# First two feed-forward blocks of chunk 0 filled by quarters of 128 tokens

## The chip, the cores and the metric

The kernel runs on one core of a Trainium2 chip. The metric is device time in microseconds (us), from the start of the program to its end; a time "of the kernel" is the median of several executions. TensorE (PE) does the matmuls, VectorE (DVE) and ScalarE (ACT) read its results out of PSUM, GpSimd (POOL) works in SBUF only, SyncE (SP) issues transfers. Transfers are issued by SP, ACT and POOL; those of POOL can change the type on the way (float32 in memory to bf16 in SBUF), those of SP and ACT do not.

## The reference

Attention with a decay and a causal mask over 8 batches, 8 heads, 576 positions, 64 per head; its output is the input of a gated feed-forward network over all 4608 tokens.

```python
# attention, q k v: (8, 8, 576, 64), s: (8, 8, 576), all float32
scores = q @ k.T / sqrt(64)
cum = cumsum(max(s, 0), axis=-1)
scores = where(causal, -1e9, scores + min(-(cum_q - cum_k), 0))
attn = softmax(scores)                       # with + 1e-9 in the denominator
x = (attn @ v) as (4608, 512)                # heads side by side
# feed-forward: w_gate, w_val (512, 1536), w_out (1536, 512), rms_g (512)
xn = x / sqrt(mean(x * x) + 1e-6) * rms_g
out = (silu(xn @ w_gate) * (xn @ w_val)) @ w_out
```

## The kernel before

**Two pipelines laid into each other.** The feed-forward runs over 9 chunks of 512 tokens (function `ffn(c)`). Within a chunk it goes over 12 blocks (fb) of 128 of the 1536 inner features. For a block, four matmuls make the gate bank Gp (L946) and four the val bank Vp (L955), each 128 x 512 in PSUM and summed over the 512 inputs. ScalarE computes Tanh of the gate (tile T, L949); VectorE makes U = (T + 1) * Gp (L958) and Ht = U * Vp (L951). Then four row tiles of output are made from the 12 blocks (L972), copied out by ScalarE and stored. Gate, val and output banks, and some others, come from one ring of four PSUM banks (`psF`); a bank is free again when U (gate) or Ht (val) has read it. Further banks: `psS` (two), `psAV` and `psT`, one each.

Between the groups of matmuls `ffn` calls `step()`, which advances a counter, the **slot** (36 per chunk, two per block and three per row tile of output). In each slot a planner in the code (not on the chip) places a piece of attention for the tokens that come next: S (scores of 128 keys by 256 queries, then Exp on ScalarE and a mask on POOL), AV (attention times v, followed on VectorE by the division into x_sb), T (transposes of q and k by TensorE, four 128x128 matmuls and a copy) and XT (the transposes of scaled x into xnT). The functions `can_s`, `can_av`, `can_t` say from which slot on a piece may be placed. Transfers, casts and checks stand in queues (`v_side`, `pool_side`, `act_side`, `dve_side`); `put(queue, n, ...)` lets an entry run from slot n on. All of it becomes one fixed order of instructions per engine, and each engine works through its own strictly in order.

**The beginning.** Batch 0 is done ahead of chunk 0 in an order written out by hand: loads, casts to bf16, transposes, scores, AV for quarters 0 to 3 of 128 tokens, each followed by the sum of squares (`norms`, ScalarE) and `alpha` (POOL: the factor 1/rms). Then, with TensorE kept busy by filler matmuls whose results nobody reads (`warm`, L849): for each quarter qb, `x_scale` (VectorE, L484) writes xs_sb, `do_xt` transposes it on TensorE into a psF16 bank (L504) and ScalarE copies it into xnT (L511), followed by two filler matmuls. Then come g_row (a copy by ScalarE), `check_mag` and two `check_max` of q of batch 0 on VectorE (L516, L522, a running maximum for a check of the value range), a one-element memset into wg_sb on VectorE (L1206), and chunk 0. Gate matmuls of chunk 0 read all four quarters of xnT.

**Loads around it.** v of batch 0 comes in five pieces; `fold_v` multiplies each with its decay factor (POOL, L417). Weights come by `load_w(src, dst, f0, f1)` from POOL, blocks f0 to f1: gate 0 to 4 and val 0 to 6 ahead of the first x, gate 4 to 6 behind the last `alpha`, gate 6 to 12 at slot 1 (behind the memset L1206, which writes into its place), val 6 to 9 and 9 to 12 at slot 3, w_out at slot 11. q and k of batch 1 come as float32 into kq32 through SP (L137) in four transfers of 512 KB: k and q of heads 0 to 3, then k and q of heads 4 to 7, behind four one-element memsets on VectorE (L1183). They are cast to bf16 (kqn) from slot 2 on: k of heads 0 to 3 on ScalarE (slot 2, L151), q of heads 0 to 3 on POOL (slot 4, L153), then heads 4 to 7 on both (slots 6 and 9). The transposes T of batch 1 (L203) follow two slots behind the cast that they need.

The three lines that tie an entry to a slot:

```python
def put(queue, n, *fns):
    queue.extend((lambda: slot[0] >= n, f) for f in fns)
put(act_side, 2, lambda: (piece1(ACT, 0, 0, 0, 4), done_cast(0, 0)))
```

The line numbers of the profile are those of this kernel:

Of the kernel before, what the change touches and what calls it, by code (L numbers as in the profile page):

```python
# [26 lines left out]
def kernel(  # L27
# [500 lines left out]
    K2 = 33  # L528
    slot = [0]
# [156 lines left out]
    def do_t(key, **kw):  # L686
# [97 lines left out]
    def can_s():  # L784
# [9 lines left out]
        if b == 1 and (phase() < 24 and phase() % 2 == 0 or kb == 4 and at("AV", 1, 3, 1) > slot[0]):  # L794
            return False
# [13 lines left out]
    def can_av(clear=False):  # L809
# [5 lines left out]
        if b >= MB and last["XS"] == slot[0]:  # L815
            return False
# [119 lines left out]
    def ffn(c):  # L936

        x0 = (c * DM) % RING
        first[0], chunk[0] = slot[0], c
        Ht = mp.tile([128, FB, DM], BF16, name="Ht", tag="Ht", bufs=2)  # L940
        pend = None
        for fb in range(FB):
            fs = slice(fb * 128, (fb + 1) * 128)
            Gp = psF()
            for cc in range(CC):
                nc.tensor.matmul(Gp, lhsT=wg_sb[:, cc, fs], rhs=xnT[:, cc, x0:x0 + DM],  # L946
                                 start=(cc == 0), stop=(cc == CC - 1))
# [4 lines left out]
            step(tanh=True)  # L952
            Vp = psF()
            for cc in range(CC):
                nc.tensor.matmul(Vp, lhsT=wv_sb[:, cc, fs], rhs=xnT[:, cc, x0:x0 + DM],  # L955
                                 start=(cc == 0), stop=(cc == CC - 1))
# [4 lines left out]
            if fb < FB - 1:  # L961
                step()
# [17 lines left out]
        for tb in range(4):  # L980
            store(tb, [(0, 384), (384, 512)] if c == NCH - 1 and tb == 3 else [(0, DM)])

# [83 lines left out]
    with tc.manual_schedule():  # L1066
# [47 lines left out]

        def stir(n):
# [65 lines left out]
        for g in (0, 1):  # L1181
            for w in (0, 1):
                nc.vector.memset(kq32[0:1, w, 4 * g, 0:1], 0.0)  # L1183
        for g in (0, 1):
            for w in (0, 1):
                load_kq(nc.sync, 1, w, 4 * g, 4 * g + 4)
# [258 lines left out]
```

## Time and profile before

| | us |
|---|---|
| median of 3 runs | 356.08 (355.93 to 356.49) |
| the profiled execution | 355.58 |
| its span (first to last instruction) | 354.1 |
| TensorE busy in it | 340.6 (96%) |
| VectorE, ScalarE, POOL busy | 276.9, 213.4, 204.5 |
| first gate matmul of chunk 0 starts at | 26.44 |

Times in the profile count from the start of the span. "PE psF L946" is work of TensorE on line 946 that writes a psF bank; PEld are the weight loads of TensorE, which run beside its matmuls. Matmuls overlap, so a matmul of 128 x 512 is listed with 0.38 us though four in a row advance by 0.86. The queue q0 (software_dynamic) carries what POOL issues, q1 what SP issues and q10 what ACT issues; a weight load is listed with the size that it has in SBUF.

### The profile page before, as it was taken

The numbers are of one execution on the slowest core, as the hardware profiler recorded it, in microseconds if no ns is written. First come the engines' busy times: TensorE is split into PE (matmuls) and PEld (weight loads), VectorE is DVE, ScalarE is ACT, GpSimd is POOL, SyncE is SP. The second block draws the span as 40 slices with busy tenths as digits, with TensorE's granted clock in tenths as the row PEclk, the third lists the DMA queues.
The fourth block names the chain that finished last, engine by engine and source line by source line (L and its number), as shares of the span: only waits on it lengthen the run. The fifth ranks groups of instructions, "written<-read, shape, count | busy, mean of one in ns | idle before, by whom it ended". The sixth has DMA issues, their size and how long they took to land.

```text
span 354.1 us, 6889 instructions
## 1 busy us (share of the span) xinstructions
PE 340.6 (96%) x2374; PEld 165.3 (47%) x2419; DVE 276.9 (78%) x524; ACT 213.4 (60%) x471; POOL 204.5 (58%) x337
## 2 busy tenths in 40 slices
PE   5989999999999999999999999999999999999995
PEld 2445444544444444444554454444544554444443
DVE  6697989598967887798889887988798659836840
ACT  3988885878786546855677557654565445224321
POOL 6969754456769986687597987597745310000000
PEclk9999999999999999999999999999999999999999
DMA  7999999999969998999899999495510121020002
GB/s 220 142 213 270 180 175 259 181 211 181 98 123 177 146 179 118 233 141 202 143 170 105 117 131 185 46 113 90 143 29 17 57 94 23 0 91 30 0 34 93
DMA packets 130528, 45.68 MB, mean 129 GB/s; under 512 B 110548, under 2 KB 125656, under 8 KB 130488
## 3 DMA queue, kind: packets, MB, share of 16 engines
q0 software_dynamic: 67056, 13.70, 50.5%
q1 hardware_dynamic: 53792, 24.20, 33.3%
q10 hardware_dynamic: 9640, 7.29, 8.2%
q8 instruction: 20, 0.33, 0.4%
q14 instruction: 20, 0.16, 0.2%
HBM read 37.90 MB, written 9.44 MB: 134 GB/s over the span
## 4 chain that ended last, share of the span: by engine, by line
PE 77%; DVE 8%; POOL 4%; issue 4%; DMA 3%; ACT 2%; SPq 0%; DVEq 0%; POOLq 0%; ACTq 0%
PE psF L972 25%; PE psF L955 21%; PE psF L946 20%; DVE U L958 2%; PE psAV L443 2%; DMA kq<-in_q_dram 2%; DMA kqT<-kqn 2%; PE psS L286 2%; DVE Ht L951 1%; PE psAV L437 1%; DVE x_sb L453 1%; PE psF L367 1%; POOL v_sb L409 1%; POOL v_sb L194 1%; PE psS L367 1%
## 5 line engine op out<-in xcount | busy, mean ns | idle before, releaser
L955 PE MATMUL psF<-xnT,wv_sb 128*128 128x512 bf16 x424 | 109.9, 379 | 0.4
L946 PE MATMUL psF<-xnT,wg_sb 128*128 128x512 bf16 x414 | 109.0, 379 | 1.3 <-ACT xnT L511 0.3
L949 ACT ACTIVATE T<-psF 128x512 f32<-128x512 f32 x108 | 64.6, 598 | 62.9 <-PE psF L946 58.8
L972 PE MATMUL psF<-wout_sb,Ht 128*128 128x512 bf16 (+2 forms) x428 | 98.9, 373 | 1.4 <-issue 0.8
L958 DVE SCALAR_TENSOR_TENSOR U<-T,psF 128x512 bf16<-128x512 f32 x108 | 73.7, 682 | 24.1 <-ACT T L949 23.9
L951 DVE TENSOR_TENSOR Ht<-U,psF 128x512 bf16<-128x512 bf16 x99 | 67.8, 685 | 6.9
L972 PEld LDWEIGHTS <-Ht 128*128 128x128 bf16 x444 | 40.1, 98 | 43.5 <-issue 1.4
L955 PEld LDWEIGHTS <-wv_sb 128*128 128x128 bf16 x432 | 39.6, 98 | 44.5 <-issue 2.9
L946 PEld LDWEIGHTS <-wg_sb 128*128 128x128 bf16 x432 | 39.4, 98 | 42.9 <-issue 2.4
L976 ACT ACTIVATE osb<-psF 128x512 f32<-128x512 f32 (+2 forms) x37 | 21.7, 587 | 58.4 <-PE psF L972 50.8
L384 POOL TENSOR_SCALAR_AFFINE_SELECT E<-E 128x512 bf16<-128x512 bf16 (+1 forms) x50 | 34.8, 704 | 28.5 <-ACT E L380 18.7
L194 POOL DMA_DIRECT2D v_sb<-in_v_dram x40 | 35.3, 885 | 0.2 <-issue 0.2
L484 DVE SCALAR_TENSOR_TENSOR xs_sb<-x_sb,al_all,g_row 128x512 bf16<-128x512 bf16 (+1 forms) x36 | 29.6, 823 | 4.1 <-POOL al_all L477 3.9
L474 POOL TENSOR_SCALAR al_all<-ss_all 128x1 f32<-128x1 f32 (+2 forms) x39 | 11.5, 295 | 35.9 <-ACT xs_sb L461 27.9
L310 ACT ACTIVATE E<-psS,biasK 128x256 bf16<-128x256 f32 (+3 forms) x88 | 29.2, 426 | 2.6 <-PE psS L286 2.6
L453 DVE TENSOR_TENSOR x_sb<-psAV,rZ 128x256 bf16<-128x256 f32 (+1 forms) x66 | 28.0, 424 | 2.3
L522 DVE TENSOR_TENSOR acc<-acc,mag 128x1280 bf16<-128x1280 bf16 x32 | 27.3, 873 | 0.2
L477 POOL TENSOR_TENSOR al_all<-al_all,mhalf 128x1 f32<-128x1 f32 (+2 forms) x39 | 25.2, 645 | 3.2
L443 PEld LDWEIGHTS <-E 128*128 128x128 bf16 x320 | 21.7, 97 | 10.5 <-POOL E L384 0.7
L461 ACT ACTIVATE xs_sb<-x_sb 128x512 bf16<-128x512 bf16 (+1 forms) x37 | 23.3, 629 | 4.6 <-DVE x_sb L453 4.0
L409 POOL TENSOR_TENSOR v_sb<-v_sb,vwx 128x512 bf16<-128x512 bf16 x25 | 25.9, 1037 | 0.1
L443 PE MATMUL psAV<-v_sb,E 128*128 128x65 bf16 x264 | 23.8, 193 | 0.1
(136 smaller groups left out, 379.8 us busy)
## 6 DMA issues: line engine op xcount, KB each, us to landing
out_dram<-osb SPq DMA_DIRECT2D x35, 256.0 KB, 2.7
kq<-in_q_dram ACTq DMA_DIRECT2D x5, 1024.0 KB, 7.5
v_sb<-in_v_dram POOLq DMA_DIRECT2D x32, 128.0 KB, 4.9
kqn<-in_k_dram POOLq DMA_DIRECT2D x20, 128.0 KB, 5.1
kq<-in_k_dram SPq DMA_DIRECT2D x4, 512.0 KB, 5.8
kq<-in_q_dram SPq DMA_DIRECT2D x4, 512.0 KB, 7.5
wout_sb<-in_moe_w_out_dram POOLq DMA_DIRECT2D x2, 768.0 KB, 10.5
kq<-in_q_dram POOLq DMA_DIRECT2D x1, 1024.0 KB, 11.0
```

The costliest lines, as they stand in the source:

```text
L194: nc.gpsimd.dma_start(out=v_sb[0:n, b % 2, c, :, 0:64], in_=v[b, :, c * 128:c * 128 + n, :].rearrange("h p d -> p h d"))
L384: nc.gpsimd.affine_select(out=Ev, in_=Ev, pattern=[[0, 4], [1, nq]], compare_op=ALU.is_ge, fill=0.0, base=0, channel_multiplier=-1)
L409: nc.gpsimd.tensor_tensor(out=v_sb[:, b % 2, c, :, 0:64], in0=v_sb[:, b % 2, c, :, 0:64], in1=vwx[:, c, i:i + H].unsqueeze(2).to_broadcast ...
L443: nc.tensor.matmul(o, lhsT=d, rhs=v_sb[:, p, qb, h, :], start=(j == 0 and qb == 0), stop=(j == 3))
L453: nc.vector.tensor_tensor(out=xo[:, g * 256:(g + 1) * 256].rearrange("p (h d) -> p h d", h=4), in0=pv[R, :, 0:64], in1=rZ[R].unsqueeze(2). ...
L484: nc.vector.scalar_tensor_tensor(out=xs_sb[R, (b * NSC + qb) % NX, :], in0=x_sb[R, (b * NSC + qb) % NX, :], scalar=al_all[R, col:col + 1], ...
L946: nc.tensor.matmul(Gp, lhsT=wg_sb[:, cc, fs], rhs=xnT[:, cc, x0:x0 + DM], start=(cc == 0), stop=(cc == CC - 1))
L949: nc.scalar.activation(out=T, in_=Gp, func=AF.Tanh, scale=0.5)
L951: nc.vector.tensor_tensor(out=Ht[:, fb - 1, :], in0=pend[0], in1=pend[1], op=ALU.mult)
L955: nc.tensor.matmul(Vp, lhsT=wv_sb[:, cc, fs], rhs=xnT[:, cc, x0:x0 + DM], start=(cc == 0), stop=(cc == CC - 1))
L958: nc.vector.scalar_tensor_tensor(out=U, in0=T, scalar=1.0, in1=Gp, op0=ALU.add, op1=ALU.mult)
L972: nc.tensor.matmul(Op[:, p0:p1], lhsT=Ht[:, fb, tb * 128:(tb + 1) * 128], rhs=wout_sb[:, fb, p0:p1], start=(fb == 0), stop=(fb == FB - 1))
```

## The change

- Blocks 0 and 1 of chunk 0 (`EARLY = 2`) take their four banks ahead of `ffn`. A new function `quarter` does, for one quarter of tokens and for banks i0 to i1 (gate 0, val 0, gate 1, val 1), four matmuls of 128 columns into that quarter of the bank. Quarters 0 and 1 are issued between the transposes of x, quarters 2 and 3 at the beginning of `ffn(0)`.
- The transposes of x take psAV16 and psT in turn in place of psF16, and of the filler of this stretch `warm(4)` and one `warm(2)` remain.
- The slots of blocks 0 and 1 shrink from four to two: the counter starts chunk 0 at 2, and both steps are called behind block 1. Several entries move to other slots, S of batch 1 with kb = 1 stays out until slot 13, AV (1, 0, 0) until slot 16.
- Loads: val weights in 0 to 2, 2 to 6 and 6 to 12; gate weights in 0 to 4, 4 to 8 and 8 to 12; the memset L1206 goes. q and k of heads 0 to 3 of batch 1 are issued behind the first AV of quarter 1 (`load1(0)`), those of heads 4 to 7 stay where they were.
- Casts: k of heads 0 to 3 moves from ScalarE to VectorE and, as q of the same heads on POOL, ahead of slot 3. `fold_v` of piece 1 moves from POOL to VectorE, that of piece 4 ahead. The two `check_max` move from the prelude to slots 5 and 6.

The diff, cut to its core:

```diff
-                    kw["pT"] = psF16()
+                    kw["pT"] = psAV16() if hp == 1 else psF16()
...
-        if b == 1 and (phase() < 24 and phase() % 2 == 0 or kb == 4 and at("AV", 1, 3, 1) > slot[0]):
+        if b == 1 and (phase() < 24 and phase() % 2 == 0 or kb == 1 and slot[0] < 13 or kb == 4 and at("AV", 1, 3, 1) > slot[0]):
...
+        if (b, qb, g) == (1, 0, 0) and slot[0] < 16:
+            return False
...
-        first[0], chunk[0] = slot[0], c
+        first[0], chunk[0] = (slot[0] if c else 0), c
...
+            begun = c == 0 and fb < EARLY
+            if begun:
+                Gp, Vp = early_bank[2 * fb:2 * fb + 2]
+                for i in (2 * fb, 2 * fb + 1):
+                    quarter(2, i, i + 1)
+                    quarter(3, i, i + 1)
+            else:
+                Gp = psF()
...
+            if begun:
+                if fb == EARLY - 1:
+                    for _ in range(EARLY):
+                        step()
...
+    def quarter(qb, i0, i1):
+        for i in range(i0, i1):
+            ws, fs = (wg_sb, wv_sb)[i % 2], slice(i // 2 * 128, i // 2 * 128 + 128)
+            for cc in range(CC):
+                nc.tensor.matmul(early_bank[i][:, qb * 128:qb * 128 + 128], lhsT=ws[:, cc, fs],
+                                 rhs=xnT[:, cc, qb * 128:qb * 128 + 128],
+                                 start=(qb == 0 and cc == 0), stop=(qb == 3 and cc == CC - 1))
...
-        load_w(moe_w_val, wv_sb, 0, 6)
-        for c in (1, 2, 3):
+        load_w(moe_w_val, wv_sb, 0, 2)
+        for c in (2, 3, 4):
             fold_v(POOL, c)
         s_first(0, 1, pairF())
         tail_step(0, psAV16())
+        fold_v(DVE, 1)
...
         do_av((0, 1, 0))
+        load1(0)
...
         alpha(0, 1)
+        load_w(moe_w_val, wv_sb, 2, 6)
...
-        load_w(moe_w_gate, wg_sb, 4, 6)
+        load_w(moe_w_gate, wg_sb, 4, 8)
+        load_w(moe_w_val, wv_sb, 6, 12)
         warm(4)
         for qb in range(4):
             x_scale(0, qb, gq)
-            do_xt((0, qb), psF16())
-            warm(2)
+        do_xt((0, 0), psAV16())
+        warm(2)
+        do_xt((0, 1), psT())
+
+        for i in range(2 * EARLY):
+            early_bank.append(psF())
+        quarter(0, 0, 2)
+        do_xt((0, 2), psAV16())
+        quarter(0, 2, 4)
+        quarter(1, 0, 1)
+        do_xt((0, 3), psT())
+        quarter(1, 1, 4)
         nc.scalar.activation(out=g_row, in_=gq, func=AF.Copy)
-        check_mag(0, 1)
-        check_max(0)
-        nc.vector.memset(wg_sb[0:1, 0, DF // 2:DF // 2 + 1], 0.0)
-        check_max(1)
...
+        piece1(POOL, 1, 0, 0, 4)
+        done_cast(1, 0)
+        piece1(DVE, 0, 0, 0, 4)
+        done_cast(0, 0)
+        check_mag(0, 1)
+        put(dve_side, 5, lambda: check_max(0), lambda: (check_max(1), done.__setitem__(("check", 0, 1), slot[0])))
...
-        put(act_side, 2, lambda: (piece1(ACT, 0, 0, 0, 4), done_cast(0, 0)))
         put(act_side, 6, lambda: piece1(ACT, 0, 1, 0, 2))
-        put(pool_side, 2, lambda: fold_v(POOL, 4))
-        put(pool_side, 4, lambda: (piece1(POOL, 1, 0, 0, 4), done_cast(1, 0)))
-        put(pool_side, 6, lambda: (piece1(POOL, 0, 1, 2, 4), done_cast(0, 1)))
+        put(pool_side, 5, lambda: piece1(POOL, 0, 1, 2, 4))
+        put(pool_side, 7, lambda: done_cast(0, 1))
...
-        put(v_side, 1, lambda: load_w(moe_w_gate, wg_sb, 6, 12))
-        put(v_side, 3, lambda: (load_w(moe_w_val, wv_sb, 6, 9), load_w(moe_w_val, wv_sb, 9, 12)))
-        put(v_side, 5, lambda: (load_tail(0), load_tail(1)))
-        put(v_side, 7, lambda: (load_v(1, 0), load_v(1, 1)))
+        put(v_side, 3, lambda: load_w(moe_w_gate, wg_sb, 8, 12))
+        put(v_side, 7, lambda: (load_tail(0), load_tail(1)))
+        put(v_side, 9, lambda: (load_v(1, 0), load_v(1, 1)))
...
+        slot[0] = 2 * EARLY - 2
         check(0, (0,))
```

More of the change, by code (lines that the diff above doesn't have):

```diff
@@ L951, in ffn @@
                 nc.vector.tensor_tensor(out=Ht[:, fb - 1, :], in0=pend[0], in1=pend[1], op=ALU.mult)
[L952 to L956, printed above, removed]
+            if not begun:
+                step(tanh=True)
+                Vp = psF()
+                for cc in range(CC):
+                    nc.tensor.matmul(Vp, lhsT=wv_sb[:, cc, fs], rhs=xnT[:, cc, x0:x0 + DM],
+                                     start=(cc == 0), stop=(cc == CC - 1))
             U = mp.tile([128, DM], BF16, name="U", tag="U", bufs=2)
@@ L1180 @@
         norms += [do_av((0, 2, 1), psT32(), act=True, apart=True)]
[L1181 to L1186, printed above, removed]
+        load1(1)
         norms[2](False)
```

21 lines of the change are left out of this document (13 added, 8 removed).

## Prediction

> **What bounds the kernel now.** I read the page first, then the stages, then the chain of waits around the start of the feed-forward. The page:
>
> ```profile
> PE 340.6 (96%) x2374; PEld 165.3 (47%) x2419; DVE 276.9 (78%) x524; ACT 213.4 (60%) x471; POOL 204.5 (58%) x337
> ...
> DMA  7999999999969998999899999495510121020002
> ```
>
> TensorE is busy for 96% of the span, so a change pays only where it takes TensorE time away. The row DMA adds the second half: for the first 60 us the transfers are as full as TensorE. By stages (columns: stretch, its length, busy time of each engine, granted clock, DMA share, GB/s):
>
> ```profile
> 20.00:26.44 6.44, 5.12 (x58) 2.90 (x56) 6.14 (x19) 4.98 (x13) 3.33 (x8) 1.00 1.09 235
> ```
>
> Only before 26.44 does TensorE have room, and there part of its 5.12 us is filler. The chain of waits shows the handover (start, length, what):
>
> ```profile
> 25.10 0.43 PE psF L849 x2
> 25.53 0.24 PE psF L504 x4
> 25.79 0.60 ACT xnT L511
> ...
> 26.44 1.02 PE psF L946 x4
> 27.46 0.86 PE psF L955 x4
> 28.33 0.86 PE psF L946 x4
> 29.19 0.22 PE psS L286 x8
> 29.41 0.97 PE psF L955 x4
> 30.38 0.22 PE psT L203 x4
> ```
>
> The first gate matmul (L946) starts when the last quarter of xnT (L511) is copied; until then TensorE runs transposes (L504) and filler (L849). From 26.44 on it runs without a gap, and among the first two blocks stands nothing but one S step (L286). What the start saves thus reaches the end, as long as nothing else becomes late.
>
> **The change part by part.** Rows of the timeline (start, length, engine, line, operation, out<-in, number; in brackets the idle time before), and from the page the weight loads of the gate:
>
> ```profile
> 10.50 1.58 DVE L153 CAST kqn<-kq 128x256 bf16<-128x256 f32 x4
> ...
> 16.26 0.80 POOL L985 DMA_DIRECT2D wv_sb<-in_moe_w_val_dram  x1
> ...
> 17.08 3.08 POOL L417 TENSOR_TENSOR v_sb<-v_sb,vw 128x520 bf16<-128x520 bf16 x3
> ...
> 17.22 0.18 DVE L451 RECIPROCAL rZ<-psAV 128x4 f32<-128x4 f32 x1 [1.36 <-PE psAV L443]
> ...
> 18.83 0.42 DVE L453 TENSOR_TENSOR x_sb<-psAV,rZ 128x256 bf16<-128x256 f32 x1
> ...
> 21.55 0.39 SPq L137 DMA_DIRECT2D kq<-in_k_dram  x1
> ...
> 22.54 2.76 DVE L484 SCALAR_TENSOR_TENSOR xs_sb<-x_sb,al_all,psS 128x512 bf16<-128x512 bf16 x4
> ...
> 23.77 2.62 ACT L511 ACTIVATE xnT<-psF 128x512 bf16<-128x512 bf16 x4 [0.39 <-PE psF L504]
> ...
> 24.24 0.84 POOL L985 DMA_DIRECT2D wg_sb<-in_moe_w_gate_dram  x1
> ...
> 25.22 0.82 DVE L516 TENSOR_SCALAR mag<-kqn 128x2560 uint16<-128x2560 uint16 x1
> ...
> 26.07 1.57 DVE L522 TENSOR_TENSOR acc<-acc,mag 128x1280 bf16<-128x1280 bf16 x2
> ...
> 31.12 1.42 POOL L153 CAST kqn<-kq 128x256 bf16<-128x256 f32 x4
> ...
> 31.53 1.03 PE L955 MATMUL psF<-xnT,wv_sb 128*128 128x512 bf16 x4
> ...
> 35.08 1.03 PE L946 MATMUL psF<-xnT,wg_sb 128*128 128x512 bf16 x4
> ...
> 44.48 0.29 PE L443 MATMUL psAV<-v_sb,E 128*128 128x65 bf16 x4
> ```
>
> ```profile
> L946 PEld LDWEIGHTS <-wg_sb 128*128 128x128 bf16 x432 | 39.4, 98 | 42.9 <-issue 2.4
> ```
>
> *Quarters.* Blocks 0 and 1 become 64 matmuls of 128x128 by 128. Before shows none of that accumulating form; the nearest are the transposes of the same shape, 0.22 us for four. Bounds: 0.21 (a quarter of L946's 0.86) and 0.39 (98 ns of weight load each, nothing hidden); I take 0.22. So 16 groups cost 3.5 us against 4 x 0.86 = 3.44: nothing by itself. The copies in L511 come 0.65 apart (2.62 / 4), so the first quarter is there at 24.4. TensorE then does: quarter 0 of two banks to 24.9, transpose 2 to 25.1, the other two banks to 25.5, one group of quarter 1 to 25.75, transpose 3 to 26.0, three groups to 26.6. Transpose 3 is 0.4 later than at 25.53, its copy ends at 26.8 instead of 26.4, and one group of quarter 2 covers that. Eight groups are left after 26.6: 1.76, to 28.4; with the S step 28.6 to 28.7, where before stood 30.38. **That is 1.7 us.** It leaves out six of the eight warm fillers in this stretch. The skipped slots 1 and 2 had no attention matmuls (chain above), so nothing is pushed back.
>
> *VectorE.* Removed from the prelude: two maxima, 1.57, which return at slots 5 and 6. Added: the four casts of k, 1.58, behind the scales that end at 25.3. With the magnitude (0.82) VectorE is free at 27.7, before Tanh of block 0 ends at about 28. No loss, if k is there at 25.3. The wait for k is new here: behind it stand the magnitude, U and Ht, and behind U the bank for block 2's gate; k later than 25.6 costs TensorE the same time. fold_v of chunk 1 on VectorE lies in its 1.36 us idle before 17.22; bounds 0.42 (half as wide, L453) and 1.03 (POOL, 3.08 / 3), either is hidden, so I take zero. If v is there only when POOL used it, 17.1, the x chain loses up to 0.8.
>
> *ScalarE* loses four casts (such as POOL's 1.42), POOL one fold; both have room, so zero (a gain of 0.1 at the second AV step at most). POOL's casts of q (1.42) move ahead of slot 3 and wait for q; behind them stand POOL's mask and the next weight loads. The transposes T of batch 1 begin one slot earlier; with slot 7 left empty, one T (0.22) fewer than before lies ahead of block 4.
>
> *Loads.* The first half of k and q is issued behind x_sb at 18.83 instead of at 21.55, about 2.1 us earlier. Val weights are cut 2 / 4 / 6 blocks, gate weights 4 / 4 / 4, and the memset by which the second gate load waited for VectorE goes. Landings and volumes (last column: us from issue to landing, issues at 16.26 and 24.24 for the first two, 21.55 for the third, 23.16 for q's second half and 34.5 for v; then packets, MB and share of the queues for 21 to 33.5 us):
>
> ```profile
> wv_sb<-in_moe_w_val_dram POOLq DMA_DIRECT2D x1, 768.0 KB, 9.7
> wg_sb<-in_moe_w_gate_dram POOLq DMA_DIRECT2D x1, 256.0 KB, 8.2
> kq<-in_k_dram SPq DMA_DIRECT2D x1, 512.0 KB, 5.8
> kq<-in_q_dram SPq DMA_DIRECT2D x1, 512.0 KB, 13.0
> v_sb<-in_v_dram POOLq DMA_DIRECT2D x1, 128.0 KB, 8.8
> ```
>
> ```profile
> q0 software_dynamic: 1244, 1.32, 63.0%
> q1 hardware_dynamic: 2068, 2.06, 52.0%
> ```
>
> Val 0 to 6 landed at 26.0. A third of it, the rest moved at that pace (1.32 + 2.06 MB in 12.5 us; weights count as bf16 here and are read as f32, so 4.7 MB read, 0.38 MB/us), lands 2.6 to 2.8 us earlier, at 23.3; it is wanted at 24.65, and as transposes 2 and 3 stand behind it, later costs one for one: 1.3 if it came at 26.0. k lands 1.4 behind val as before (27.35 against 25.95), at 24.8, in time; the end of that bound is 27.35, as now, which costs 1.75. Val 2 to 6 wants to be there at 31.53 - 1.7 + 0.22 = 30.1; behind k and q it lands at 29 to 30.5. I take no loss.
>
> **Gate 4 to 8 is the one that doesn't fit.** Block 4's gate starts at 35.08 before; with 1.7 less, and one T fewer ahead of it, it would start at 33.2. Now it needs all four blocks of the load issued at about 24.3, not two. By then must have crossed since 21: val 0 to 6 (0.79), gate 4 to 8 (0.52) and k and q (2.1): 1.31 and 2.1 MB. That is what crossed by 33.5 before, with the queues full throughout. With 0.5 for the last bytes (val: last packets at 25.5, landed at 26.0) it lands at 34.0; earliest 32.6, if all of q's second half (0.5 MB) is overtaken; latest 35.0, if slow engines straggle. So TensorE waits about 0.8 to 0.9 there.
>
> *Sum.* 1.7 - 0.9 = **0.8 us**. A second limit confirms the size: v of batch 1 lands at 34.5 + 8.8 = 43.3, and its first use was at 44.5 (L443); the same bytes go ahead of it now, so more than 1.2 could not be kept. The profiled execution took 355.58 us (span 354.1 and 1.5 around it), which becomes 354.8; it lies 0.5 below the median 356.08, which becomes **355.3**.
>
> **A rule against the trace.** Who gets the engines when both queues are full? Three stretches (25.5 to 28.5; 29 to 31.5; 17 to 21, where the software queue is alone):
>
> ```profile
> q1 hardware_dynamic: 1108, 1.10, 108.7%
> q0 software_dynamic: 1, 0.00, 0.0%
> ```
>
> ```profile
> q0 software_dynamic: 429, 0.22, 63.4%
> q1 hardware_dynamic: 428, 0.43, 61.5%
> ```
>
> ```profile
> q0 software_dynamic: 509, 0.53, 92.5%
> ```
>
> In the first, gate weights issued at 24.24 got one packet beside k and q: roughly in order of arrival, which is what I used above. In the second the two alternate one for one. The Trainium skill, page "DMA: Bandwidth & Descriptors", section "Queues, rings and completion order", says that each engine goes round the queues it has work for, packet by packet. The second stretch agrees with it, the first doesn't; by that rule k and q would be held by weights all the time, and the result would be that of the slower rival below.
>
> **The rivals.**
> 1. *Loads keep up* (gate 4 to 8 overtakes q, the 1.2 of v is stretched): 1.2 to 1.7 gained, 354.5. For it: q's second half was overtaken before too (13.0, to 36.2, after gate 4 to 6 at 32.4). Against: full queues. Chance 0.15.
> 2. *The gain is eaten whole*, by gate 4 to 8 at 34.9 or k at 27.3: within 0.3 of before, 356.0. Chance 0.1.
> 3. *Slower: k and q starve.* Val 2 to 6, gate 4 to 8 and val 6 to 12 now queue without the gap that the memset made. If they alternate one for one at the software queue's own pace (509 packets in 4 us, 127 per us), the 1024 packets of the first half (1 MB at the 1 KB of the first stretch) take 8.1 us, from 22.1 if they start 2.7 behind their issue: landed at 30.7, cast by POOL at 32.1, where T in slot 5 wants it at 30.0. That eats 2.1. k's second half needs 4 us more, to 34.7; ScalarE stands at its cast in slot 6 with Tanh of block 3 behind it, about another 1. Net 1.4 slower, 357.4; it decides from a landing of q past 30.3. For it: the second stretch. Against: the first, and that k and q are issued ahead of those weights. Chance 0.25.
>
> That the quarters do not overlap at all (xnT waited for as a whole) would give +0.1 and the same loads as in 2; I count it there.
>
> **How the numbers follow.** The forecast has 0.5, its own range 354.9 to 355.8 (0.3 to 1.2 gained). Faster by over 0.2% means over 0.7 us, about what a measurement of this kernel can tell from no change: 0.31 of the forecast and rival 1, 0.46. Within 0.2%: 0.19 of it and most of rival 2, 0.28. Slower: 0.26. The range leaves out 0.05 below 354.2 and 0.12 above 357.4.
>
> **What would show it.** Right: the first matmul of the quarters at 24.4 to 24.5, the S step of slot 3 near 28.5, TensorE idle before block 4's gate with gate weights named, that gate at about 34.0. Wrong: VectorE idle before its casts beyond 25.6; POOL or ScalarE idle for k or q; or no wait at block 4, which makes it rival 1; or a group of quarters at 0.39, which would take back 1.4 after 26.6.

## The result and the profile after the change

The changed kernel takes **358.79 us** in the median of 10 executions (357.18 to 360.39), the kernel before 356.36 us in 10 beside it (355.58 to 357.91). The ratio is 1.0071, 95% interval 1.0057 to 1.0086: **slower by 2.4 us**, where the forecast was 0.8 us faster. The profiled execution took 357.18 us (span 355.7, before 354.1); it is the fastest of the ten, so it shows about 1.6 us of the loss, and a second profile (below) more. In one kernel below, the quarters alone, four of six executions were over 2% longer than its fastest, at a lower granted clock of TensorE; its times are therefore given apart.

The page of the changed kernel:

```profile
PE 343.4 (97%) x2461; PEld 167.4 (47%) x2461; DVE 278.5 (78%) x528; ACT 212.2 (60%) x467; POOL 204.3 (57%) x336
...
DMA  7999999899959999999999999296810131020002
...
q8 instruction: 20, 0.33, 0.5%
```

TensorE has 87 matmul and 42 weight load records more (the cut blocks are 48 matmuls more, each with its weight load, and six fillers fewer: 84 instructions; some records of before are missing). The last row is a queue that will matter below: 20 packets, 0.33 MB. The two stretches of the start after the change (length, busy time of PE, PEld, DVE, ACT, POOL, clock, DMA share, GB/s), and then the second one before it:

```profile
20.00:26.44 6.44, 5.42 (x82) 4.09 (x82) 5.87 (x20) 4.68 (x11) 5.22 (x10) 1.00 1.11 269
26.44:36.00 9.56, 8.67 (x99) 5.58 (x98) 8.25 (x15) 6.69 (x14) 7.74 (x14) 1.00 1.18 234
```

```profile
26.44:36.00 9.56, 9.51 (x72) 5.01 (x73) 6.92 (x13) 7.78 (x18) 8.78 (x15) 1.00 1.18 267
```

The second stretch is the news: before, TensorE was busy for 9.51 of these 9.56 us; now it stands for 0.9. The timeline of that stretch names what it waits for (below it, the gate of block 2 in the kernel before):

```profile
22.88 2.78 DVE L484 SCALAR_TENSOR_TENSOR xs_sb<-x_sb,al_all,psS 128x512 bf16<-128x512 bf16 x4
24.76 0.38 PE L1003 MATMUL psF<-xnT,wg_sb 128*128 128x128 bf16 x4
24.98 0.39 PE L1003 MATMUL psF<-xnT,wv_sb 128*128 128x128 bf16 x4
...
25.58 1.08 DVE L153 CAST kqn<-kq 128x256 bf16<-128x256 f32 x4
...
26.82 1.85 POOL L153 CAST kqn<-kq 128x256 bf16<-128x256 f32 x4 [0.66 <-DMA kq<-in_q_dram]
...
28.87 0.29 PE L286 MATMUL psS<-kqT 64*128 64x64 bf16 x8
29.55 1.03 PE L957 MATMUL psF<-xnT,wg_sb 128*128 128x512 bf16 x4
...
31.28 1.04 PE L967 MATMUL psF<-xnT,wv_sb 128*128 128x512 bf16 x4 [0.39 <-DMA wv_sb<-in_moe_w_val_dram]
...
35.01 1.04 PE L957 MATMUL psF<-xnT,wg_sb 128*128 128x512 bf16 x4 [0.50 <-DMA wg_sb<-in_moe_w_gate_dram]
```

```profile
30.44 1.03 PE L946 MATMUL psF<-xnT,wg_sb 128*128 128x512 bf16 x3
```

Four matmuls of a quarter take 0.22 us (24.76 to 24.98), the casts of k on VectorE wait for nothing, the gate of block 2 begins at 29.55 instead of 30.44. Then val of block 2 waits 0.39 and the gate of block 4 0.50; that gate starts at 35.01, where it started at 35.08 before. **By block 4 the start's gain is gone.** The chain of waits of the whole execution holds three transfers from here on (start, length, what):

```profile
24.57 10.39 DMA wg_sb<-in_moe_w_gate_dram
...
75.02 7.94 DMA kqT<-kqn
...
162.90 6.92 DMA kqT<-kqn
```

The last two lie far behind the change, in a part of the program whose instructions and their order are those of before. What TensorE waits for from 67 us on (in total, times, longest), after:

```profile
PE psF L367 <- DMA kqT<-kqn: 0.9, 1, 0.9
PE psS L286 <- DMA kqT<-kqn: 0.4, 1, 0.4
```

In before the same view names no wait of TensorE for kqT. Matched weight load by weight load, the changed kernel is 0.15 us behind before at the first gate of chunk 1 (67.41 against 67.26), 0.7 behind from 83 us and 1.7 behind from 169 us to the end.

### The profile page after: what moved, and what is told of

It reads as the page before. It is cut to its first block, busy times and chain, and to the rows that moved or that the text cites. A ratio compares the mean times of both kernels' runs of the same rounds, so it can differ in the third digit from the quotient of the medians.

```text
span 355.7 us, 7020 instructions
## 1 busy us (share of the span) xinstructions
PE 343.4 (97%) x2461; PEld 167.4 (47%) x2461; DVE 278.5 (78%) x528; ACT 212.2 (60%) x467; POOL 204.3 (57%) x336
## 4 chain that ended last, share of the span: by engine, by line
PE 77%; DMA 7%; POOL 4%; DVE 4%; ACT 3%; issue 3%; SPq 0%; POOLq 0%; DVEq 0%; ACTq 0%
PE psF L988 26%; PE psF L967 20%; PE psF L957 19%; DMA kqT<-kqn 4%; DMA wg_sb<-in_moe_w_gate_dram 3%; PE psAV L443 2%; PE psS L286 2%; PE psAV L437 2%; PE psF L367 1%; DVE U L970 1%; POOL v_sb L409 1%; PE psS L367 1%; DVE x_sb L453 1%; DVE Ht L962 1%; ACT E L326 1%
## 5 line engine op out<-in xcount | busy, mean ns | idle before, releaser
L988 PE MATMUL psF<-wout_sb,Ht 128*128 128x512 bf16 (+2 forms) x444 | 100.9, 374 | 0.0
L962 DVE TENSOR_TENSOR Ht<-U,psF 128x512 bf16<-128x512 bf16 x99 | 67.7, 684 | 6.8
L957 PEld LDWEIGHTS <-wg_sb 128*128 128x128 bf16 x424 | 38.6, 98 | 42.2 <-issue 1.9
L461 ACT ACTIVATE xs_sb<-x_sb 128x512 bf16<-128x512 bf16 (+1 forms) x37 | 23.3, 629 | 4.3 <-DVE x_sb L453 3.7
L319 POOL TENSOR_SCALAR_AFFINE_SELECT E<-E 128x512 bf16<-128x512 bf16 x19 | 13.1, 691 | 19.2 <-ACT E L310 18.6
```

Source lines behind the costliest of these rows:

```text
L962: nc.vector.tensor_tensor(out=Ht[:, fb - 1, :], in0=pend[0], in1=pend[1], op=ALU.mult)
L988: nc.tensor.matmul(Op[:, p0:p1], lhsT=Ht[:, fb, tb * 128:(tb + 1) * 128], rhs=wout_sb[:, fb, p0:p1], start=(fb == 0), stop=(fb == FB - 1))
```

## The experiments

Two theories stood at the beginning. *Start*: the loads that were recut are late, and what is late at the start is carried to the end. *Later*: the start is about even, and something far behind it has become slower. A third one came up on the way: *pieces*, told below.

### The same kernel again

> The changed kernel once more, for a second profile. In the first, block 4's gate waited for gate weights 4 to 8 (they landed at 35.0), chunk 1 began 0.15 us later than before, and 1.5 us more were lost behind that, at two waits for kqT transposes (by 0.5 us at 83 and by 1.0 at 169). Theory A (loads at the start, and chance behind it): block 4's gate again near 35.0, chunk 1 again near 67.6, but the later losses elsewhere or of another size. Theory B (the change itself makes the transposes of batches 2 and 4 late): the same two places again, 0.5 and 1.0.

It took 357.92 us. In this execution val of block 2 waits longer, and the chain shows why:

```profile
21.70 11.01 DMA wv_sb<-in_moe_w_val_dram
```

Val 2 to 6 lands at 32.7, 1.4 later than in the first profile, and TensorE waits 1.64 for it; it is 1.3 behind before at the first gate of chunk 1, loses 0.2 at 83 and 0.7 at 169 us. So both kinds of loss are there in both executions, in changing shares.

### Quarters alone, and loads alone

The first has the quarters with the loads, casts, fold and maxima of before (val still cut 2 / 4):

```diff
-        for c in (2, 3, 4):
+        for c in (1, 2, 3):
             fold_v(POOL, c)
...
-        fold_v(DVE, 1)
...
         do_av((0, 1, 0))
-        load1(0)
...
+        load1(0)
         load1(1)
...
-        load_w(moe_w_gate, wg_sb, 4, 8)
-        load_w(moe_w_val, wv_sb, 6, 12)
+        load_w(moe_w_gate, wg_sb, 4, 6)
...
-        piece1(POOL, 1, 0, 0, 4)
-        done_cast(1, 0)
-        piece1(DVE, 0, 0, 0, 4)
-        done_cast(0, 0)
...
+        put(act_side, 2, lambda: (piece1(ACT, 0, 0, 0, 4), done_cast(0, 0)))
+        put(pool_side, 4, lambda: (piece1(POOL, 1, 0, 0, 4), done_cast(1, 0)))
```

> Quarters, the two skipped slots, and val weights cut at block 2 as in the change; all other loads, casts, folds and checks as before. Theory A: gate 4 to 6 (256 KB) lands near 32.5 as before, block 4's gate is not held and starts about 1.5 us earlier than before; 0.9 to 1.5 us faster than before in all. Rival (the quarters gain nothing, because the casts and transposes of batch 1 can't come earlier): within 0.4 us of before. Theory B, if the shift of chunk 0 is what makes the later transposes late: up to 1.5 us slower than before.

The second has everything but the quarters (`EARLY = 0`, x transposed in one row as before):

> Loads, casts, folds and checks of the change without the quarters: blocks 0 and 1 in four slots, as before. Theory A: gate 4 to 8 lands near 35.0, just when block 4's gate starts in before (35.1), so 0 to 0.3 us lost there, and in all within 0.7 us of before. Theory B, if the recut loads are what makes later work late: 1.5 to 2.5 us slower, as the whole change.

Quarters alone: **359.64 and 363.30 us** in two executions, 367.36 to 370.65 in the four others (before 356.09). Loads alone: 356.89, ratio 1.0023 (1.0007 to 1.0038). The quarters without the recut loads are worse than anything forecast, already in the two shortest (3.6 and 7.2 us above before), so the recutting is there for a reason: ScalarE stands at the cast of k's second half with Tanh behind it. The profile of quarters alone (its fastest execution):

```profile
22.54 11.05 DMA kq<-in_k_dram
```

k lands at 33.6, after ScalarE has stood idle for 2.2 us, and TensorE comes to need it earlier than before. This profile also has the later waits for kqT, loads alone has none of them. That was the first hint that the later loss goes with the quarters.

### Before, started later

Four fillers more behind the last transposition of x (0.86 us of TensorE, of which 0.25 was idle before):

```diff
-            warm(2)
+            warm(2 if qb < 3 else 6)
```

> The kernel before with four more filler matmuls (0.86 us of TensorE) ahead of chunk 0. If a shift of the start goes through to the end unchanged: 0.86 us slower, and the waits for kqT as before. If later waits depend on where the chunk falls against the transfers (both theories allow it as chance): anything from 0.2 less to 2 us more.

356.4 us, ratio 1.0005 (0.9992 to 1.0019). The profile is 0.75 to 0.85 behind before all the way from 27 us to the end, with no loss on top: 0.35 because x came later in this execution (its first transposition at 23.69, before at 23.34), 0.44 by the fillers. So a shift in time by itself does not make kqT late. The median is 0.3 behind, in keeping with the 0.44.

### Where the instructions come from

Three transfers in 74 to 84 us, by the view of DMA issues (last column: median us from issue to landing), before and after:

```profile
q8 instruction: 1, 0.02, 0.7%
...
v_sb<-in_v_dram POOLq DMA_DIRECT2D x2, 128.0 KB, 5.5
...
kqT<-kqn SPq DMA_TRANSPOSE x3, 5.4
xnT<-xs_sb SPq DMA_TRANSPOSE x1, 5.4
```

```profile
q8 instruction: 1, 0.02, 0.6%
...
v_sb<-in_v_dram POOLq DMA_DIRECT2D x3, 128.0 KB, 6.7
...
kqT<-kqn SPq DMA_TRANSPOSE x3, 7.0
xnT<-xs_sb SPq DMA_TRANSPOSE x1, 7.7
```

These three are slower, and so is a load of q of 128 KB (6.0 to 7.7); in the same view v of 64 KB (7.2 to 6.0) and a load of q of 1024 KB (8.6 to 7.0) are quicker. The same view gives GB/s in 40 slices of 0.75 us for 60 to 90 us, before and then after:

```profile
GB/s 335 345 241 112 232 313 194 12 384 292 0 142 255 127 75 152 229 295 356 351 216 154 152 147 157 174 182 194 96 112 168 319 329 315 200 173 51 38 30 102
```

```profile
GB/s 324 347 257 315 127 8 207 303 278 393 47 60 304 146 62 161 165 351 344 328 276 144 155 44 24 147 161 144 135 105 179 196 265 348 347 331 201 56 11 28
```

In slices 24 and 25 (77.25 to 78.75 us) after drops to 44 and 24 where before moves 147 and 157. One thing is different just ahead of it: the queue named "instruction" has one packet of 16 KB in 74 to 84 us in both, but its place differs. In 60 to 90 us each kernel has two of them; the record of packets has them at 64.2 and 80.7 us before, at 62.5 and 75.7 after. (The expectations below give such places 0.5 us later, 81.3 for 80.7.) In the changed kernel the second piece lies in the burst of v's small packets and the transposes. The whole program has 20 such pieces in either kernel.

Hence the third theory: q8 brings TensorE's instructions, a piece for so many of them. The change adds 84 instructions, so each later piece comes some 2 to 8 us sooner, and one that falls among other transfers delays them. To test it without the change, the fillers are cut into narrower ones, the same TensorE time in more instructions:

```diff
     def warm(n):
         ps = psF()
         for i in range(n):
-            nc.tensor.matmul(ps, lhsT=ident_bf, rhs=mneg, start=True, stop=True)
+            recut(ps, 4)
+
+    def recut(ps, n):
+        w = DM // n
+        for j in range(n):
+            nc.tensor.matmul(ps[:, j * w:j * w + w], lhsT=ident_bf, rhs=mneg[:, j * w:j * w + w],
+                             start=True, stop=True)
```

Four pieces each for `warm` and the second `stir` give before 84 instructions more; eight each (`recut(ps, 8)`, one filler with four) give 168 for `warm` alone, and with `stir` 258 more than before in both kernels. Cut into four, the fillers take the time that they took whole: from the first transposition of x to the last 2.06 us against 2.02, and 1.07 against 1.08 from there to the first gate.

> The kernel before with 14 of its 512-column filler matmuls cut into four of 128 columns: the same filler time, and 84 TensorE instructions more, as many as the change adds; nothing else differs. Theory A (the queue q8 brings TensorE's instructions in pieces of 16 KB; the extra 84 rows move all later pieces about 5 us earlier, and the piece that stood at 81.3 us falls at 76 among the transfers of v and kqT and holds them up): chunk 1 begins within 0.2 us of before, kqT transposes in 74 to 84 us take about 7.0 instead of 5.4 us to land, TensorE waits for kqT near 83 and 169, the span grows by 0.5 to 1.5 us, time 356.8 to 357.9. Theory B (the quarters shift stores, loads of batch 2 and casts against each other, instruction pieces do not matter): kqT stays at 5.4 us, time within 0.3 of before.

> The changed kernel with its 13 512-column fillers cut into pieces of 64 columns (one of them 128), so that TensorE has 174 instructions more, 258 more than before: the pieces of 16 KB fall one whole piece further, at before's places. Theory A: kqT in 74 to 84 us lands in about 5.4 us again, the losses at 83 and 169 us (0.5 and 1.0) go, time 357.0 to 357.9 against 358.8 of the change; the waits at val of block 2 and gate of block 4 stay. Theory B: the losses stay, 358.5 to 359.0.

> The kernel before with its fillers cut finer still (258 TensorE rows more, as many as in the recut of the changed kernel): the pieces of 16 KB move by one whole piece and two rows, so they fall where they fell before, one more in all. Theory A (the place of the pieces decides): kqT in 74 to 84 us at 5.4 us, no loss at 83 and 169, time within 0.4 of before. If cutting the fillers itself, or a longer stream, cost the 3.3 us of the first recut: 358 to 360.

> The kernel before with 168 TensorE rows more (fillers at the start of the feed-forward cut into 64 columns): the pieces move by two thirds of their distance of 17 us, the one of 81.3 us to about 70, the next to 87. Theory A: none falls between 74 and 80 us, so kqT there takes 5.3 to 5.8 us and nothing is lost at 83 us; at 160 to 170 us the pieces stand at about 158 and 176, so nothing is lost there either: time within 0.6 of before. If the loss grew with the length of the stream: 84 rows cost 3.3 us, so 168 would cost more than that, 359 to 363.

What came out (the places of the pieces from the record of packets, the landings of kqT from the view of DMA issues):

| kernel | TensorE instructions more | piece near 78 us | kqT, 74 to 84 | piece near 167 us | kqT, 158 to 171 | median us | ratio to before |
|---|---|---|---|---|---|---|---|
| before | 0 | 80.7 | 5.4 | 169.8 | 5.6 | 356.1 to 356.4 | |
| loads alone | 0 | 81.1 | 5.3 | 169.4 | 5.4 | 356.89 | 1.0023 (1.0007 to 1.0038) |
| after | 84 | 75.7 | 7.0 | 166.5 | 7.2 | 358.79 | 1.0071 (1.0057 to 1.0086) |
| before, recut | 84 | 76.5 | 6.7 | 166.0 | 7.3 | 359.49 | 1.0087 (1.0068 to 1.0107) |
| before, recut | 168 | 67.7, 87.5 | 5.2 | 157.7 | 6.5 | 358.92 | 1.0088 (1.0058 to 1.0118) |
| before, recut | 258 | 81.6 | 5.8 | 170.3 | 5.7 | 356.23 | 1.0002 (0.9988 to 1.0015) |
| after, recut | 258 | 81.1 | 5.4 | 169.5 | 5.2 | 356.80 | 1.0017 (1.0002 to 1.0033) |

**84 instructions more for the same fillers, and nothing else, make the kernel before 3.3 us slower; 258 more cost nothing.** So neither the cutting nor the length of the stream costs time, but the place of the pieces: 258 instructions move them on by one whole piece. The 3.3 us are more than the 0.5 to 1.5 that I expected; four of its six executions, at a mean granted clock of 0.993 to 0.995, took 359.5 to 360.1, the two at 1.0 took 357.9 and 358.4 (1.8 and 2.2 above before). In the recut kernel before the transfers drop as they do after the change:

```profile
GB/s 255 285 333 250 173 206 76 47 267 79 367 311 183 229 112 93 121 134 319 370 358 281 145 154 43 25 44 157 155 146 225 179 205 303 350 348 285 197 32 0
```

Slices 25 to 27 (78.0 to 80.25 us), right behind its piece of 76.5 to 77.5, have 43, 25 and 44. And TensorE waits for kqT from 67 us on:

```profile
PE psF L367 <- DMA kqT<-kqn: 1.6, 2, 0.9
```

Both waits stand near 169 us; at 83, where this execution arrives 1.0 later than before, it loses only 0.1. In the second profile of the change, too, the loss at 169 is there, though the median of its kqT in 158 to 171 us is only 5.0. In the changed kernel the recut to 258 takes 2.0 us off the median, and its profile has no wait for kqT left. The expectation for 168 was half wrong: at 74 to 84 us the transfers are fast, as expected, but I looked at that place and the one at 170 only. A piece at 103.9 now falls among transposes of x (a wait of 0.4 there, and 0.6 lost), one at 157.7 just ahead of the kqT of 163 (6.5 us, and 1.1 lost at 169). Where a piece is harmless must be seen for the whole program.

The record of packets shows the same in every profile. In all six in which a piece begins between 74.9 and 77.6 us, some packets of v (128 bytes, otherwise 32 ns) that begin 1.2 to 1.6 us behind it hang for up to 1.5 us; in the changed kernel they are 30, begun from 77.2 to 77.6, and all end at 78.7. Of the 13 profiles without a piece there, 12 have no such packet from 70 to 84 us, and one has three, of 0.4 us.

How the piece delays the others was not tried by itself. It takes 0.99 us in the changed kernel and is over at 76.7; from 77.8 to 78.6 us only 10 to 15 packets start in each 0.2 us instead of some 230, about what one of the 16 engines does at that rate. That would fit a backlog on the piece's engine on which what comes next has to wait; it is not shown.

### The weight loads

The two that TensorE waited for, cut to when they are wanted:

```diff
-        load_w(moe_w_val, wv_sb, 2, 6)
+        load_w(moe_w_val, wv_sb, 2, 4)
...
-        load_w(moe_w_gate, wg_sb, 4, 8)
-        load_w(moe_w_val, wv_sb, 6, 12)
+        load_w(moe_w_gate, wg_sb, 4, 6)
+        load_w(moe_w_val, wv_sb, 4, 6)
...
-        put(v_side, 3, lambda: load_w(moe_w_gate, wg_sb, 8, 12))
+        put(v_side, 3, lambda: (load_w(moe_w_gate, wg_sb, 6, 9), load_w(moe_w_val, wv_sb, 6, 9)))
+        put(v_side, 5, lambda: (load_w(moe_w_gate, wg_sb, 9, 12), load_w(moe_w_val, wv_sb, 9, 12)))
```

> The changed kernel with its weight loads cut to when they are wanted: val 2 to 4 instead of 2 to 6; gate 4 to 6 and val 4 to 6 instead of gate 4 to 8 and val 6 to 12; then gate and val 6 to 9 in slot 3 and 9 to 12 in slot 5. If the start's gain was lost to the size of these two loads: val 2 to 4 lands about 1.3 us earlier than val 2 to 6 (31.3 to 32.7 in the two profiles), gate 4 to 6 about 2.6 earlier than gate 4 to 8 (34.96), no wait at blocks 2 and 4, chunk 1 begins 1.2 to 1.7 earlier than before, and the time is 357.2 to 357.7 with the later losses still there. If the queues are simply full whatever the order: waits move to other loads (gate 6 to 9, v of batch 1), chunk 1 begins within 0.4 of before, 358.3 to 358.9.

357.8 us, ratio 1.0046 (1.0030 to 1.0062): 1.0 less than the change. The waits at blocks 2 and 4 are gone: TensorE is busy for 9.51 of the 9.56 us again, and 0.9 ahead of before at block 4 although x came 0.8 late in this execution.

```profile
26.44:36.00 9.56, 9.51 (x114) 6.43 (x113) 8.48 (x16) 7.40 (x17) 8.42 (x15) 1.00 1.29 247
```

But in the waits from 20 to 67 us stands:

```profile
PE psAV L443 <- DMA v_sb<-in_v_dram: 1.2, 1, 1.2
```

v of batch 1, now behind all the weights, takes the gain back at 45 us. Neither expectation had this quite: the size of the loads was the cause of the two waits, and the next load in the full queues became late, as the prediction's second limit said.

### The fold

`fold_v(DVE, 1)` taken out, chunk 1 folded on POOL and chunk 4 in slot 2, as before:

> The changed kernel with the fold of v's chunk 1 back on POOL and chunk 4's fold in slot 2, as before. If the 1.68 us on VectorE delay the first normalization: x scale begins about 0.3 us earlier, val 2 to 6 and gate 4 to 8 wait no less (their landing is set by the queues), so 0 to 0.3 faster, 358.5 to 358.8. If the fold was hidden: no difference.

358.03 us, ratio 1.0059 (1.0036 to 1.0082); in the median 0.8 less than the change, with intervals that overlap. In the profile of the change the fold stands right ahead of the first normalization (below it, before's matmuls of the same place):

```profile
15.87 1.68 DVE L417 TENSOR_TENSOR v_sb<-v_sb,vw 128x520 bf16<-128x520 bf16 x1
...
17.23 0.30 PE L443 MATMUL psAV<-v_sb,E 128*128 128x65 bf16 x4
...
17.56 0.18 DVE L451 RECIPROCAL rZ<-psAV 128x4 f32<-128x4 f32 x1
```

```profile
16.88 0.30 PE L443 MATMUL psAV<-v_sb,E 128*128 128x65 bf16 x4
```

It takes 1.68 us, longer than the upper bound of 1.03. The reciprocal, at 17.22 before, follows at 17.56, but the matmuls whose result it reads are 0.35 late too (17.23 against 16.88), so it is these that set it here. In the eight profiles with this fold on VectorE it takes 0.70 to 1.96 us, and only two of them have the reciprocal later behind its matmuls than before has it, by 0.2 (second profile of the change) and 0.4 us (finer loads without quarters, below). Why its time varies is open.

Without it the profiled execution is 0.8 ahead of before at block 4, the forecast's figure, and 0.6 at chunk 1 (66.67 against 67.26), and then loses 0.5 at 83 and 1.0 at 169 us, as the change does. That this comes from the fold is not shown: the first transposition of x begins at 23.2 here, and at 23.3 to 23.9 in five profiles of before and its variants, which all have the fold on POOL. The next runs show no gain by the fold on top of the others.

### All together

First the fold on POOL and the fillers recut (258), then the finer loads as well, with v of batch 1 in slot 5, gate and val 9 to 12 in slot 7 (`put` says 6, loads go out in odd slots), the tails in slot 9:

```diff
+        put(v_side, 5, lambda: (load_v(1, 0), load_v(1, 1)))
+        put(v_side, 6, lambda: (load_w(moe_w_gate, wg_sb, 9, 12), load_w(moe_w_val, wv_sb, 9, 12)))
+        put(v_side, 9, lambda: (load_tail(0), load_tail(1)))
```

> The changed kernel with the fold of chunk 1 back on POOL and the fillers recut (258 rows more than before). If the fold and the place of the pieces are the two losses beside the loads: chunk 1 begins 0.3 to 0.9 us earlier than before and nothing is lost later, 355.2 to 355.9. If the recut alone did it: the same as that, 356.8.

> As the last, and the weights cut to when they are wanted (val 2 to 4; gate 4 to 6, val 4 to 6; gate and val 6 to 9 in slot 3), v of batch 1 in slot 5 ahead of gate and val 9 to 12 in slot 6, the tails in slot 9. If the size of the loads took the gain of the quarters (1.7 us): no wait at blocks 2, 4 and at the first v of batch 1, chunk 1 begins 1.2 to 1.7 us earlier than before, 354.3 to 355.0. If the queues are full and something else is then late (v, tails, gate 9 to 12): 355.3 to 356.2.

356.82 us (1.0019, 1.0003 to 1.0035), no better than the recut alone, and 356.21 (0.9994, 0.9975 to 1.0013). The first still waits for weights (1.4 us for val 2 to 6, 0.6 for gate 4 to 8 in its profile). In the second no weight is late, but POOL, which now issues more loads and still does the fold of chunk 4 in slot 2, comes late with its casts:

```profile
PE psT L203 <- POOL kqn L153: 1.3, 2, 0.9
```

So the fold goes back to where the change had it (VectorE does chunk 1's), or POOL keeps chunk 1's and VectorE does chunk 4's in slot 2:

> The changed kernel (fold of chunk 1 on VectorE as there) with the fillers recut (258 rows more than before) and the weights cut to when they are wanted, v of batch 1 in slot 5, gate and val 9 to 12 in slot 7, the tails in slot 9. If the three losses found so far (size of the loads, place of the pieces, 0.3 us of the fold) are all, and POOL's casts of q are no longer held up by a fold and a load ahead of them: no wait of TensorE above 0.5 us between 26 and 67 us, chunk 1 begins 0.7 to 1.3 us earlier than before, nothing lost later, 354.8 to 355.5. If full queues or POOL's loads eat it again: 355.9 to 356.5, like the version with the fold on POOL.

> As the last, with chunk 1's fold on POOL and chunk 4's on VectorE in slot 2 instead. If the fold on VectorE ahead of the first normalization costs 0.3 us: 0.2 to 0.4 earlier than the last, 354.5 to 355.2. If VectorE's fold now holds up U and Ht of block 1 or 2: TensorE waits for a bank of U there, 0.5 to 1.0 later.

**355.44 us, ratio 0.9965 (0.9941 to 0.9989)**: this version beats both kernels. With the fold of chunk 4 on VectorE instead it is 355.8 (0.9979, 0.9952 to 1.0006), no gain by that. To see whether it is the quarters or the finer loads that gain, the same loads without quarters (`EARLY = 0`), and the best version once more beside them:

> The version without quarters (loads, casts, fold and checks of the change) with the finer loads: val 2 to 4, gate and val 4 to 6, 6 to 9, v of batch 1, 9 to 12, tails. Its TensorE rows are before's within a few, so the pieces stay in place. If the quarters are worth what fine_recut gained: no gain here, 356.2 to 356.9, 0.8 to 1.4 behind fine_recut. If the finer loads alone brought fine_recut below before: 355.3 to 355.7, like fine_recut.

> The same kernel as fine_recut, on the same chip as loads_fine: 355.1 to 355.9, and a profile without the wait of 1.7 us for xnT at 67.7 us that its first profile showed, if that was chance; with it, if the start's gain meets the transposes of x there.

Finer loads without quarters: 356.46 (1.0013, 0.9999 to 1.0028). With them: 355.84 (0.9984, 0.9970 to 0.9998). With the same loads the quarters make the difference, 0.6 us here. In both profiles of the best version TensorE is 0.9 ahead of before at the gate of block 4 and 0.7 ahead from block 5 to 44 us, and then meets the next limit at the first gate of chunk 1, the transposes of chunk 1's x. In the two (first, again):

```profile
PE psF L963 <- DMA xnT<-xs_sb: 1.7, 1, 1.7
```

```profile
PE psF L963 <- DMA xnT<-xs_sb: 0.7, 1, 0.7
```

So the start's gain is more than given back there in these two executions, whose spans are 354.9 and 354.3 against 354.1 before. The first is the slowest of its twelve (356.40, median 355.44), the second stands in the middle of its twelve (355.82, median 355.84). How much of the gain the others keep, their times alone tell; no profile shows it.

### Quarters alone, recut

> The quarters with the loads and casts of before (368.8 us) and the fillers recut as above. If the place of the pieces caused its ten lost microseconds: 356 to 359. If they come from the cast of k on ScalarE that stands ahead of Tanh: 365 to 370 still.

363.52 us (361.68 to 366.88; ratio 1.019, 1.0133 to 1.0246), 7 above before. The two shortest executions of quarters alone took 359.64 and 363.30, so whether the recut gained anything here can't be told. Behind 46 us its profile loses nothing more against before, where that of quarters alone loses 2.0, with waits for kqT. Its loss lies at the start (idle time and what ended it in brackets):

```profile
37.94 0.72 ACT L151 ACTIVATE kqn<-kq 128x256 bf16<-128x256 f32 x2 [5.67 <-DMA kq<-in_k_dram]
...
39.20 0.21 PE L437 MATMUL psAV<-v_sb,E 128*128 128x65 bf16 x1 [3.96 <-ACT kqT L211]
...
41.34 1.91 PE L963 MATMUL psF<-xnT,wg_sb 128*128 128x512 bf16 x4
```

ScalarE stands 5.7 us at the cast of k's second half, and TensorE 4.0 behind it. The wait costs a second time: from 37.8 to 44.6 us the granted clock of TensorE is 0.50 in this profile, and the four matmuls of a gate (last row) take 1.91 us instead of 1.03. Why k lands at 37.9 here and at 33.6 in the other profile is open.

## Why the prediction was wrong

**Quarters: right.** I said 0.22 us for four matmuls and 1.7 us by the S step of slot 3. In the execution whose x came on time (the fold on POOL; first transposition at 23.23, before at 23.34), the timeline of TensorE has

```profile
28.42 0.29 PE L286 MATMUL psS<-kqT 64*128 64x64 bf16 x8
28.64 0.40 PE L203 MATMUL psT<-ident_bf,kqn 128*128 128x128 bf16 x4
28.88 0.39 PE L203 MATMUL psAV<-ident_bf,kqn 128*128 128x128 bf16 x4
29.10 1.03 PE L957 MATMUL psF<-xnT,wg_sb 128*128 128x512 bf16 x3
...
34.25 1.04 PE L957 MATMUL psF<-xnT,wg_sb 128*128 128x512 bf16 x4 [0.75 <-DMA wg_sb<-in_moe_w_gate_dram]
```

The S step ends at 28.64, as said (28.6 to 28.7). Two transposes T follow instead of one, so block 2's gate begins 1.34 earlier than before (29.10 against 30.44). The last row is block 4's gate: here the forecast of the start came out, a wait of 0.75 for gate 4 to 8 (said 0.8 to 0.9) and 0.83 ahead of before (34.25 against 35.08).

**Casts of k on VectorE: right.** They began at 25.58 with no wait. POOL's wait for q was 0.66, hidden.

**The fold on VectorE: wrong in its bound, mostly right in its price.** The step "bounds 0.42 and 1.03, either is hidden" took two rows that were no bounds of it: 0.70 to 1.96 us were measured, 1.68 in the first profile. It delayed the first normalization in two of eight profiles, by 0.2 and 0.4 us, and not in the first one.

**Val 2 to 6: mis-sized.** "I take no loss": it landed at 31.3 and 32.7 in the two profiles instead of 29 to 30.5, waits of 0.39 and 1.64. **Gate 4 to 8: right place, 1.0 too early.** It landed at 34.96 in the first profile and not at 34.0, at the end of my bound (35.0), and that eats the rest. Both landings vary from execution to execution: with these loads, val landed at 29.9 to 32.7 and gate at 34.2 to 35.9 in five profiles, so my figures were the early end. One reason is in the volumes for 21 to 33.5 us; I had set 1.31 MB of weights by 33.5, as before. After:

```profile
q0 software_dynamic: 1341, 1.17, 57.9%
q1 hardware_dynamic: 2102, 2.09, 56.0%
```

As much of k and q, but 0.15 MB less of the weights, which had 57.9% of the queues' time instead of 63.0. At the pace of 27 to 32 us (0.61 MB in 5 us, below) 0.15 MB are 1.2 us by my estimate: about the size of the miss.

**Who gets the engines: my reading was wrong.** I took the transfers to go "roughly in order of arrival". After, from 27 to 32 us:

```profile
q0 software_dynamic: 616, 0.61, 72.4%
q1 hardware_dynamic: 592, 0.59, 43.4%
```

About one packet of one queue for one of the other. The Trainium skill, page "DMA: Bandwidth & Descriptors", section "Queues, rings and completion order", says so (each engine goes round the queues it has work for, packet by packet), and this trace agrees, 616 to 592. What I took for order of arrival was a late beginning: the weights issued at 24.24 before had their first packets of 512 bytes at 28.7, and after the change val 2 to 6, issued at 21.37, its first of 1024 bytes at 25.0. As long as the load hadn't begun, the other queue had the engines for itself (1108 packets to 1 in the prediction's first stretch). The rival that drew on this (k and q starve) still didn't come true as described: the first halves were there in time. It was the weights that the alternation held back; what part of the 0.15 MB is due to it wasn't tried.

**"What the start saves thus reaches the end, as long as nothing else becomes late": this step failed.** The condition was the question, and I looked for what becomes late only among the transfers that the change moves. The profile of before had the row of the instruction queue; I gave the 84 instructions no price. They cost more than the start was to gain: 2.0 us of the median of the changed kernel (358.79 to 356.80 by the recut; 3.3 us in the kernel before). The finer loads are worth another 1.4 (356.80 to 355.44; 1.0 by the second run of that version, 355.84). Those two are 3.0 to 3.4 of the 3.5 us by which the forecast of 355.3 missed. That the version without them lands so near the forecast is in part luck: it also moves v and the tails, and in both of its profiles the start's gain is gone at the first gate of chunk 1.

## What to carry to other kernels

Where a kernel is near its limit, count the instructions that a change adds to an engine's stream, and look where the pieces of the instruction queue fall against the transfers that the engine waits for; a few fillers more or fewer can be worth more than the change, and a control with the same work in another number of instructions tells it in one run. Where the queues are full, cut each load to what is wanted next and follow the next two loads behind it: a saved wait goes to them first (here val and gate, then v, then POOL's casts, then x of chunk 1). A loss far behind the change, in code that did not change, is a reason to look at what the engines share, not at the code there.

## What the runs showed of the hardware

- TensorE's instructions come during the run, in packets of 16,384 bytes on the queue q8, 13 to 21 us apart from 43 to 283 us of the changed kernel; 258 instructions more move them by about one packet, and 16,384 / 258 is 63.5 bytes. The Trainium skill, page "Trainium Architecture — The Big Picture", section "The software stack", gives 64 bytes for an instruction, which agrees. Each packet takes 0.88 to 2.3 us on its engine. Where one met bursts of small packets and transposes, most of these landed 1.2 to 2.3 us later (v of 128 KB 5.5 to 6.7, kqT 5.4 to 7.0, xnT 5.4 to 7.7), and some packets of v hung for up to 1.5 us.
- A weight load issued on POOL had its first packet 3.6 and 4.5 us after the issue while the queues were full (21.4 to 25.0 after, 24.24 to 28.7 before).
- The same `128x520` product of v took 1.07 us on POOL in the kernel before (first piece) and 0.70 to 1.96 us on VectorE in eight profiles; what sets it there is open.
- In the quarters alone recut TensorE waited from 35.2 to 39.2 us; the granted clock was 0.50 from 37.8 to 44.6, and four matmuls of 128 x 512 took 1.91 us instead of 1.03.
